# Hand-woven issue order for a linear-attention and mixture-of-experts kernel, with plainly loaded weights cast on chip

## The chip, the cores and the metric

The kernel runs on one core of one Trainium2 chip. The metric is the device time of one execution in microseconds (us). A few executions are timed for each kernel, beside executions of the kernel before on the same chip. Of each run one execution was recorded as a profile. A timed run counts as slow when it is over 1.5% above the fastest of the same kernel, and ratios use the others, the fast ones, alone. Five engines work in parallel (in the profile of the kernel before, the busy times of the first four below add up to 511.6 us in a span of 278.8): TensorE (PE; its weight loads are PEld), VectorE (DVE), ScalarE (ACT), GpSimd (POOL) and SyncE (SP, which here only issues transfers). Each has its own instruction list, and in the traces below an instruction waits behind those ahead of it in its list (in experiment 5, ScalarE's copy of kvT, whose transposes were issued at 76.9 us, stood behind casts until 83.1 us). A "session" below is one visit to one chip.

## The reference

Linear attention over 8 batches, 8 heads, 576 positions and 64 channels per head, followed by a mixture of 8 experts in which each row goes to the one expert with the largest logit. Cut to what matters:

```python
q_s = softmax(q, over channels)
k_s = softmax(k, over positions)
kv  = einsum('bhsd,bhse->bhde', k_s, v)      # 64 x 64 per head
x   = einsum('bhsd,bhde->bhse', q_s, kv)     # 4608 rows of 512
logits = x @ w_gate + modality_bias[modality_id]
e_idx  = argmax(logits)
for e in range(8):
    h = maximum(x[rows of e] @ w1[e], 0)     # 512 -> 1024
    out[rows of e] = gate * (h @ w2[e])      # 1024 -> 512
```

The modality bias decides nearly all routing, so the kernel loads only the two experts that the two biases name, and checks on chip that no row wanted another (a fallback loop handles the rest and did not run here).

## The kernel before

Each batch goes through `attend` (k, v and q are loaded in fp32, exponentiated or cast by ScalarE; 36 `kv` matmuls; the normaliser `kinv` on VectorE; transposes; gate logits; x) and `route` (ranks on VectorE). GpSimd then sends each row of x to its expert's half of a buffer `xd` in DRAM with indexed transfers, and SyncE fetches rows from it, transposed, for the FFN. An FFN "piece" is half of a y tile (4 matmuls of 512 columns) or a quarter of a 256-row first layer (8 matmuls of 256 columns). The scheduler orders every engine; the program only gives attention a higher priority.

```python
GW = 512                                     # columns of one FFN pass
GROUPS = [[0], [1], [2], [3], [4, 5], [6], [7]]

def attend(b, between=None):
    ...
    for hp in range(2):
        for j in range(NJ):                  # NJ = 9
            for hg in range(2):
                rows = slice(64 * hg, 64 * hg + 64)
                nc.tensor.matmul(out=kv[hg][:, 130 * hp : 130 * hp + 129],
                                 lhsT=ek[rows, j, ...], rhs=vb[rows, j, hp, 0:129], ...)
    kinv = small.tile([P, 2, 2], FP32, name="kinv")
    for hg in range(2):
        nc.vector.tensor_scalar_add(out=kinv[:, hg, :], in0=view(kv[hg], ...), scalar1=1e-9)
    ...                                      # kvbd = kv * kinv; transposes of q
    nc.tensor.transpose(out=kvT_ps..., in_=kvbd[:, p_, :], identity=ident)
    nc.scalar.copy(out=kvT, in_=kvT_ps...)   # ScalarE, needed by the gate matmul g
    ...

def load_weights(eid, s, wait=None):
    ld = nc.gpsimd.dma_start(out=W[...] (bf16), in_=moe_w1[...] (fp32))   # cast while loading
    ...

for ph, bs in enumerate(GROUPS):
    with tc.high_priority(offset=AHEAD):     # attention ahead of the FFN
        for b in bs:
            prep_k(b); prep_v(b, nc.scalar); prep_q(b)
            alone(attend(b))
            ...
        alone(route(ph))
        fetch(ph)
    for slot, lo, w in todo_of(ph):          # FFN passes of this phase
        ...
```

The softmax here doesn't subtract the row's maximum and nothing guards it: scores larger than these inputs give would overflow.

Of the kernel before, what the change touches and what calls it, by code (L numbers as in the profile page):

```python
# [42 lines left out]
def kernel(  # L43
# [28 lines left out]
    GW = 512  # L72
# [6 lines left out]
    GROUPS = [[0], [1], [2], [3], [4, 5], [6], [7]]  # L79
    FULL = [256, 512, 768, 1024, 1536, 1792, CAP]  # L80
# [15 lines left out]
    stage = ctx.enter_context(tc.tile_pool(name="stage", bufs=6))  # L96
    sb = ctx.enter_context(tc.tile_pool(name="sb", bufs=2))
    small = ctx.enter_context(tc.tile_pool(name="small", bufs=2))
    xpass = ctx.enter_context(tc.tile_pool(name="xpass", bufs=4))
    info = ctx.enter_context(tc.tile_pool(name="info", bufs=8))  # L100
    hbuf = ctx.enter_context(tc.tile_pool(name="hbuf", bufs=2))
# [10 lines left out]
    manual = ExitStack()  # L112

# [3 lines left out]
    def load_batch(b):  # L117
        for nm, src in (("k", k), ("v", v), ("q", q)):

            t = stage.tile([P, HG, NJ * Dh], FP32, name="st", tag="st")  # L120
            ld = nc.sync.dma_start(  # L121
                out=t,
                in_=bass.AP(
                    tensor=src.tensor,
                    offset=src.offset + b * H * S * Dh,
                    ap=[[NJ * Dh, P], [2 * S * Dh, HG], [1, NJ * Dh]],
                ),
            )
            st.setdefault(("dma", b), ld)
            st[nm, b] = t  # L130
# [7 lines left out]
    wg_sb = const.tile([P, KD, E], BF16)  # L138

    for h2 in range(2):  # L140
        for hl in range(2):
            nc.gpsimd.dma_start(
                out=wg_sb[64 * h2 : 64 * h2 + 64, 2 * hl : 2 * hl + 2, :],
                in_=bass.AP(
                    tensor=moe_w_gate.tensor,
                    offset=moe_w_gate.offset + (2 * h2 + hl) * Dh * E,
                    ap=[[E, Dh], [4 * Dh * E, 2], [1, E]],
                ),
            )
    mraw = const.tile([P, B, NJ, 2], I32)  # L150
    m32 = _dram_bitcast(moe_modality_id, I32)
    for hg in range(2):
        nc.sync.dma_start(  # L153
            out=mraw[64 * hg : 64 * hg + 64],
            in_=bass.AP(tensor=m32.tensor, offset=m32.offset, ap=[[2 * NJ, 64], [2 * S, B], [1, 2 * NJ]]),
        )
# [54 lines left out]
    xb_b = [persist.tile([P, NT2, RW], BF16, name=f"xb{i}") for i in range(2)]  # L211
    for xb in xb_b:
        nc.gpsimd.memset(xb[:, :, D + INF : RW], 0.0)
    aoff = persist.tile([P, B * NT + 1], FP32)
# [3 lines left out]

    key = const.tile([P, 2], FP32)
# [23 lines left out]
    def biases():  # L243

        modf = const.tile([P, B, NT], FP32, name="modf")
        nc.vector.memset(modf, 0.0)
        for hg in range(2):
            pr = (64 * hg, 64)
            nc.vector.tensor_copy(
                out=modf[64 * hg : 64 * hg + 64, :, 1:NT], in_=view(mraw, [[2 * NJ, B], [4, NT - 1]], 2 * hg, pr)  # L250
            )
        nc.vector.tensor_copy(out=modf[0:64, :, 0], in_=view(mraw, [[2 * NJ, B]], 2 * (NJ - 1), (0, 64)))
# [9 lines left out]
    W_dma = []  # L262

    def load_weights(eid, s, wait=None):

        for part in range(4):
            dst = W[:, s, part * 2 * F : (part + 1) * 2 * F]
            if part < 2:
                ld = nc.gpsimd.dma_start(
                    out=view(dst, [[F, 2], [1, F]]),  # L270
# [6 lines left out]
            else:  # L277
                ld = nc.gpsimd.dma_start(
                    out=view(dst, [[D, 4], [1, D]]),
# [6 lines left out]
            W_dma[:] = [ld]  # L286
            if wait is not None and part == 0:
                after(ld, [wait], "transfers in the order of need")
# [19 lines left out]
    def exp_of(b, nm, out):  # L308
        src = st.pop((nm, b))
        for g in range(2):  # L310
            nc.scalar.activation(  # L311
                out=view(out, [[Dh, 2], [HG * Dh, NJ], [1, Dh]], 2 * g * Dh),
                in_=src[:, 2 * g : 2 * g + 2, :],
                func=ACT.Exp,
            )

    def prep_k(b):
        eks[b] = sb.tile([P, NJ, HG * Dh], BF16, name="ek")
        exp_of(b, "k", eks[b])

    def prep_v(b, eng):
        vst = st.pop(("v", b))
        for hp in range(2):
            copy_on(
                eng,
                view(vb_b[b % 2], [[Dh, 2], [260, NJ], [1, Dh]], 130 * hp),
                view(vst, [[NJ * Dh, 2], [Dh, NJ], [1, Dh]], 2 * hp * NJ * Dh),
            )

    def prep_q(b):  # L330
        eqs[b] = sb.tile([P, NJ, HG * Dh], BF16, name="eq")
        exp_of(b, "q", eqs[b])

    def attend(b, between=None):
        kvbd, gx, et, vb = kvbd_b[b % 2], gx_b[b % 2], et_b[b % 2], vb_b[b % 2]
        ek, eq = eks.pop(b), eqs.pop(b)
        kv = [ka.tile([P, 512], FP32, name="kv_ps", tag="ka") for _ in range(2)]
        for hp in range(2):
            for j in range(NJ):
# [9 lines left out]
                if j == 4:  # L349
                    yield 1  # L350
            yield 1
# [7 lines left out]
        for hg in range(2):  # L359
            for h2 in range(2):  # L360
# [6 lines left out]
                )  # L367

        for c0, nj in ((0, 4), (4, 4), (8, 1)):
            tp = ka.tile([P, 1024], BF16, name="tp_ps", tag="ka")  # L370
# [12 lines left out]
            if nj > 1:  # L383
                yield 1
# [5 lines left out]
        yield 1  # L390
        if between:
            between()
# [7 lines left out]
        yield 1  # L400
# [24 lines left out]
        yield 1  # L425

        xb = xb_b[b // 2 % 2]
        o = b % 2 * NT
        nc.gpsimd.tensor_copy(out=view(xb.bitcast(I32), [[RW // 2, NT]], (o * RW + D) // 2 + 1), in_=id_i[:, b, :])
        for t in range(NT):  # L430
            T = tsz[t]
            x_ps = mm.tile([P, 512], FP32, name="x_ps", tag="mm")
            for p_ in range(NP):
                nc.tensor.matmul(  # L434
                    out=view(x_ps, [[2 * Dh, 2], [1, Dh]], (4 * (p_ % 2) + p_ // 2) * Dh, (0, T)),
                    lhsT=et[:, p_, tcol[t] : tcol[t] + T],
                    rhs=kvbd[:, p_, :],
                    start=True,
                    stop=True,
                )  # L440
            nc.vector.tensor_tensor(  # L441
                out=view(xb, [[2 * Dh, HG], [Dh, 2], [1, Dh]], (o + t) * RW, (0, T)),
                in0=view(x_ps, [[2 * Dh, HG], [Dh, 2], [1, Dh]], 0, (0, T)),
                in1=view(qi, [[1, HG], [HG, 2], [0, Dh]], t * H, (0, T)),
                op=ALU.mult,
            )
            yield t % 2

    lws, part_of = {}, {}
    ROWS = "rows of their own"  # L450

    def route(ph):
# [5 lines left out]
        xb = xb_b[b // 2 % 2]  # L458
        R2 = RW // 2
        col = (b % 2 * NT * RW + D) // 2  # L460
# [27 lines left out]
        yield 1  # L488
# [40 lines left out]
        for i in bs:  # L529
            for t in range(NT):  # L530
                c = (i - b) * NT + t
                T = tsz[t]
                w = nc.gpsimd.indirect_dma_start(  # L533
                    out=xd,
                    out_offset=bass.IndirectOffsetOnAxis(ap=place[0:T, c : c + 1], axis=0),
                    in_=xb[0:T, i % 2 * NT + t, :],
                    in_offset=None,
                    bounds_check=NSLOT - 1,
                    oob_is_err=False,
                )  # L540
                tc.declare_no_dep(w.ins, group="sent", reason=ROWS)
                tc.add_to_no_dep_group("sent", w.ins)
                part_of.setdefault(ph, []).append(w)
        yield 0
# [64 lines left out]
    def fetch(ph):  # L609
        for slot, lo, w in todo_of(ph):  # L610
# [5 lines left out]
            got["dma"] = d  # L616
# [4 lines left out]
    def ffn1(w, slot, xt, hT):  # L621

        nf = GW // w
        for f0 in range(0, KF, nf):
            h_ps = ff.tile([P, GW], FP32, name="h_ps", tag="ff")
# [51 lines left out]
    def main_pieces():  # L677

        before = None
        for ph in range(NPH):  # L680
            for slot, lo, w in todo_of(ph):
# [3 lines left out]
                if before:  # L685
                    yield from second(*before)
                before = (ph, lo, w, slot, hT, ti)
        yield from second(*before)

    main = main_pieces()  # L690

    def weave(side):
        for n in side:
            for _ in range(n):
                next(main, None)

    def alone(side):
        for _ in side:
            pass


    AHEAD = 4000
    a0 = attend(0)
    with tc.high_priority(offset=AHEAD):
        prep_k(0)
        prep_v(0, nc.scalar)
        prep_q(0)
        for _ in range(5):
            next(a0)
        gating()  # L710
    eids = nc.values_load_multi_w_load_instructions(
        eid_i[0:1, 0:2],
        engines=[ENG.Pool],
# [4 lines left out]
    load_weights(eids[0], 0)  # L718
    load_batch(2)
    after(st["dma", 2], W_dma, "transfers in the order of need")  # L720
    for ph, bs in enumerate(GROUPS):
        with tc.high_priority(offset=AHEAD):
            for b in bs:
                if b:
                    prep_k(b)
                    prep_v(b, nc.scalar)
                    prep_q(b)
                    alone(attend(b))
                else:
                    alone(a0)  # L730
                    biases()
                if ph and b + 3 < B:
                    load_batch(b + 3)
            alone(route(ph))
            if ph == 0:
                load_weights(eids[1], 1, part_of[0][-1])
            if ph == NPH - 1:
                fill_gap()
            fetch(ph)
            if ph == 0:  # L740
                load_batch(3)
                after(st["dma", 3], [got["dma"]], "transfers in the order of need")
# [89 lines left out]
```

## Time and profile before

| | before |
|---|---|
| median of the timed runs, first session | 287.61 us (286.82 to 287.75) |
| the execution that was profiled | 280.36 us, span 278.8 us |
| TensorE, VectorE, ScalarE, GpSimd busy | 194.2, 113.4, 111.3, 92.7 us |
| mean granted TensorE clock | 0.931 |

The span runs from the first instruction to the last. The profiled execution was 7 us faster than the timed ones; it is not one of them, and the record does not say in which session it was taken. The line below is from the page of the kernel before: the clock that was granted to TensorE in 40 equal slices, in tenths.

```profile
PEclk9999999999959999689979899999799999999955
```

Only a few slices fall below full speed (the clock records of this profile begin at 62.5 us; what lies before counts as full).

### The profile page before, as it was taken

What the parts mean: (1) busy time and instruction counts of PE and PEld (TensorE: products, weight loads), DVE (VectorE), ACT (ScalarE), POOL (GpSimd) and SP (SyncE); (2) the same over time, 40 slices, a digit from 0 to 9 for tenths busy, and PEclk for the clock granted to TensorE, in tenths of its full rate; (3) what the DMA queues carried; (4) which work ended last, traced back from release to release, by engine and by line L of the source; (5) the groups of instructions that cost most, each with busy time, mean ns of one, the idle gap of its engine ahead of it and who ended that gap; (6) DMA issues with size and microseconds to landing.
All of it is one profiled execution on the core that took longest, in us unless ns stands there. A gap on an engine that the chain in (4) does not pass through costs nothing.

```text
span 278.8 us, 4469 instructions
## 1 busy us (share of the span) xinstructions
PE 194.2 (70%) x1627; PEld 119.8 (43%) x1647; DVE 113.4 (41%) x415; ACT 111.3 (40%) x148; POOL 92.7 (33%) x128
## 2 busy tenths in 40 slices
PE   0242554368479899298579498994999999999400
PEld 0232333146355667167346274542446644446200
DVE  1253373525555968239728286203212221213100
ACT  1643338314378686276356122250242333331100
POOL 7610024402510171262375073273514221414200
PEclk9999999999959999689979899999799999999955
DMA  7999969796999995997994724335534220303000
GB/s 184 337 283 283 244 228 375 121 196 139 389 407 334 226 406 146 331 369 119 316 355 142 148 92 127 102 112 141 183 75 152 95 94 2 144 0 153 14 5 0
DMA packets 47580, 52.75 MB, mean 189 GB/s; under 512 B 28655, under 2 KB 30719, under 8 KB 47552
## 3 DMA queue, kind: packets, MB, share of 16 engines
q1 hardware_dynamic: 38816, 33.45, 41.0%
q0 software_dynamic: 8736, 18.95, 23.3%
q8 instruction: 15, 0.25, 0.4%
q14 instruction: 13, 0.11, 0.1%
HBM read 36.88 MB, written 15.25 MB: 187 GB/s over the span
## 4 chain that ended last, share of the span: by engine, by line
PE 37%; DMA 19%; DVE 13%; issue 13%; SPq 7%; POOL 3%; ACT 2%; POOLq 0%; DVEq 0%; ACTq 0%
PE y_ps L645 17%; PE h_ps L628 15%; DMA ti<-xd 8%; DVE xb L441 4%; DMA st<-in_v_dram 4%; SPq L572 3%; DVE y_sb L655 2%; DMA st<-in_k_dram 2%; SPq L121 2%; POOL xd L533 2%; SPq L153 2%; PE x_ps L434 2%; DMA xd<-xb,place 2%; PE tp_ps L373 1%; DVE lg L463 1%
## 5 line engine op out<-in xcount | busy, mean ns | idle before, releaser
L628 PE MATMUL h_ps<-xt,W 128*128 128x256 bf16 (+2 forms) x510 | 78.4, 305 | 9.6 <-DMA xt<-xd 7.2
L635 ACT ACTIVATE hT<-h_ps 128x512 bf16<-128x512 f32 x76 | 45.2, 596 | 90.1 <-PE h_ps L628 90.1
L645 PE MATMUL y_ps<-W,hT 128*128 128x512 bf16 x286 | 72.9, 394 | 7.7 <-DVE y_sb L655 3.6
L533 POOL DMA_INDIRECT xd<-xb,place x40 | 38.8, 970 | 86.4 <-issue 34.5
L628 PEld LDWEIGHTS <-W 128*128 128x128 bf16 x512 | 48.7, 102 | 33.5 <-issue 12.3
L658 POOL DMA_INDIRECT out_dram<-y_sb,ix x38 | 37.0, 974 | 67.2 <-DVE y_sb L655 48.0
L655 DVE TENSOR_SCALAR y_sb<-y_ps,ti 128x512 f32<-128x512 f32 x38 | 28.2, 746 | 57.2 <-PE y_ps L645 54.4
L645 PEld LDWEIGHTS <-hT 128*128 128x128 bf16 x304 | 28.7, 100 | 37.2 <-issue 6.0
L342 PE MATMUL kv_ps<-vb,ek 64*128 64x129 bf16 x288 | 16.3, 264 | 24.2 <-ACT vb L301 24.2
L441 DVE TENSOR_TENSOR xb<-x_ps,qi 128x512 bf16<-128x512 f32 (+1 forms) x40 | 25.7, 679 | 17.2 <-PE x_ps L434 17.0
L311 ACT ACTIVATE ek<-st 128x1152 bf16<-128x1152 f32 x16 | 18.1, 1159 | 18.2 <-DMA st<-in_k_dram 18.2
L311 ACT ACTIVATE eq<-st 128x1152 bf16<-128x1152 f32 x16 | 17.7, 1156 | 12.5 <-DMA st<-in_q_dram 12.5
L373 PE MATMUL tp_ps<-ident,eq 128*128 128x128 bf16 x144 | 13.8, 241 | 12.2 <-DVE kvbd L362 6.4
L301 ACT CAST vb<-st 128x1152 bf16<-128x1152 f32 x16 | 17.7, 1156 | 11.1 <-DMA st<-in_v_dram 11.1
L342 PEld LDWEIGHTS <-ek 64*128 64x128 bf16 x288 | 11.6, 115 | 23.0 <-ACT vb L301 18.9
L434 PE MATMUL x_ps<-kvbd,et 128*128 128x128 bf16 (+1 forms) x160 | 18.4, 251 | 1.1 <-DVE xb L441 0.7
L373 PEld LDWEIGHTS <-eq 128*128 128x128 bf16 x144 | 10.7, 108 | 15.9 <-issue 6.8
L434 PEld LDWEIGHTS <-et 128*128 128x128 bf16 (+1 forms) x160 | 12.0, 112 | 11.8 <-issue 9.2
L593 DVE SCALAR_TENSOR_TENSOR m<-ti,m 128x2 f32<-128x2 int32 (+2 forms) x16 | 2.4, 157 | 32.2 <-DMA ti<-xd 32.1
L301 ACT COPY et<-tp_ps 128x1024 bf16<-128x1024 bf16 x8 | 8.1, 1010 | 6.9 <-PE tp_ps L373 6.9
L362 DVE TENSOR_TENSOR kvbd<-kv_ps,kinv 64x128 bf16<-64x128 f32 x32 | 9.1, 285 | 0.6
L398 DVE CAST gx<-g_ps 64x32 bf16<-64x32 f32 x8 | 1.4, 175 | 19.3 <-PE g_ps L395 19.3
(102 smaller groups left out, 115.2 us busy)
## 6 DMA issues: line engine op xcount, KB each, us to landing
st<-in_k_dram SPq DMA_DIRECT2D x8, 1152.0 KB, 6.8
st<-in_v_dram SPq DMA_DIRECT2D x8, 1152.0 KB, 14.4
st<-in_q_dram SPq DMA_DIRECT2D x8, 1152.0 KB, 18.1
W<-in_moe_w_dram POOLq DMA_DIRECT2D x8, 512.0 KB, 12.9
xd<-xb,place POOLq DMA_INDIRECT x40, 3.5
out_dram<-y_sb,ix POOLq DMA_INDIRECT x38, 2.7
xt<-xd SPq DMA_TRANSPOSE x16, 4.8
ti<-xd SPq DMA_DIRECT2D x10, 4.0 KB, 4.1
```

What stands on the lines that cost most here:

```text
L301: nc.scalar.copy(out=out, in_=in_)
L311: nc.scalar.activation(out=view(out, [[Dh, 2], [HG * Dh, NJ], [1, Dh]], 2 * g * Dh), in_=src[:, 2 * g : 2 * g + 2, :], func=ACT.Exp,)
L342: nc.tensor.matmul(out=kv[hg][:, 130 * hp : 130 * hp + 129], lhsT=ek[rows, j, P * hp : P * hp + P], rhs=vb[rows, j, hp, 0:129], start=(j = ...
L373: nc.tensor.transpose(out=view(tp, [[2 * nj * 64, 2], [1, 64]], hp * nj * 64 + jj * 64), in_=eq[:, c0 + jj, P * hp : P * hp + P], identity ...
L434: nc.tensor.matmul(out=view(x_ps, [[2 * Dh, 2], [1, Dh]], (4 * (p_ % 2) + p_ // 2) * Dh, (0, T)), lhsT=et[:, p_, tcol[t] : tcol[t] + T], r ...
L441: nc.vector.tensor_tensor(out=view(xb, [[2 * Dh, HG], [Dh, 2], [1, Dh]], (o + t) * RW, (0, T)), in0=view(x_ps, [[2 * Dh, HG], [Dh, 2], [1, ...
L533: w = nc.gpsimd.indirect_dma_start(out=xd, out_offset=bass.IndirectOffsetOnAxis(ap=place[0:T, c : c + 1], axis=0), in_=xb[0:T, i % 2 * NT ...
L628: nc.tensor.matmul(out=h_ps[:, f * w : (f + 1) * w], lhsT=W[:, slot, kd * F + (f0 + f) * P : kd * F + (f0 + f + 1) * P], rhs=xt[:, kd, 0:w ...
L635: nc.scalar.activation(out=hT[:, f0 : f0 + nf, 0:w], in_=view(h_ps, [[w, nf], [1, w]]), func=ACT.Relu)
L645: nc.tensor.matmul(out=y_ps, lhsT=hT[:, kf, t * P : (t + 1) * P], rhs=W[:, slot, W2 + kf * D : W2 + (kf + 1) * D], start=(kf == 0), stop=( ...
L655: nc.vector.tensor_scalar(out=y_sb, in0=y_ps, scalar1=gate[:, t, 3:4], scalar2=None, op0=ALU.mult)
L658: store = nc.gpsimd.indirect_dma_start(out=out, out_offset=bass.IndirectOffsetOnAxis(ap=ix[:, t : t + 1], axis=0), in_=y_sb, in_offset=Non ...
```

## The change

The intent is to stop leaving the order to the scheduler. A `manual_schedule` region fixes every engine's list to the order in which the program emits it. `attend` and `route` yield weights (0.7, 1.5, ...) that say roughly how long the step will keep TensorE waiting. `weave` multiplies them by a rate and places an FFN piece each time a whole one is owed. Weights come as plain fp32 transfers, four on SyncE's queue and four on ScalarE's, into staging tiles, and are cast on chip. Passes are 256 wide, each batch is its own group, and more buffers are given to staging, x passes and h.

```diff
-    GW = 512
+    GW = 256
-    GROUPS = [[0], [1], [2], [3], [4, 5], [6], [7]]
+    GROUPS = [[b] for b in range(B)]
-    stage ... bufs=6     xpass ... bufs=4     hbuf ... bufs=2
+    stage ... bufs=8     xpass ... bufs=6     hbuf ... bufs=3
+    manual.enter_context(tc.manual_schedule())
...
+    def prep(b, v_eng):                     # six casts, one per step of the weave
+        for nm in "kvq":
+            for g in range(2):
+                ...
+                yield
     def attend(b):
         for hp in range(2):
             for j in range(NJ):
                 ... kv matmuls
                 if j == 4:
-                    yield 1
+                    yield 0.7
-            yield 1
+            if hp == 0:
+                yield 0.7
...
-    ld = nc.gpsimd.dma_start(out=view(dst, ...), in_=...)
+    t = stage.tile([P, HG * NJ * Dh], FP32, name="st", tag="st")
+    eng.dma_start(out=view(t, ...), in_=...)
+    def cast_weights(s, part, eng):
+        copy_on(eng, W[:, s, part * 2 * F : (part + 1) * 2 * F], wst.pop((s, part))[:, 0 : 2 * F])
...
+    def weave(side, rate, preps=()):
+        owed = 0.0
+        for x in side:
+            next(preps, None)
+            owed += x * rate
+            while owed >= 1:
+                mains(1)
+                owed -= 1
...
+    load_batch(4)
+    weave(chain(attend(2), route(2)), 0.3, prep(3, nc.scalar))
+    fetch(2)
+    load_batch(5)
+    weave(chain(attend(3), route(3)), 0.5, prep(4, nc.scalar))
+    for b in range(4, B):
+        fetch(b - 1)
+        if b + 2 < B:
+            load_batch(b + 2)
+        weave(chain(attend(b), route(b)), 0.97, prep(b + 1, nc.scalar) if b + 1 < B else ())
+    fill_gap()
+    fetch(B - 1)
+    for _ in main:
+        pass
```

## The prediction

The sum, 72 + 2 x 16 + 4 x 22.3 + 57 + 17 + 8.7, came to 275.7 (it rounded on the way).

> **What bounds the kernel now.** I read the page's strip of 40 slices first (one digit per 7 us, in tenths busy) to see whether one thing bounds the whole.
>
> ```profile
> PE   0242554368479899298579498994999999999400
> ...
> DMA  7999969796999995997994724335534220303000
> GB/s 184 337 283 283 244 228 375 121 196 139 389 407 334 226 406 146 331 369 119 316 355 142 148 92 127 102 112 141 183 75 152 95 94 2 144 0 153 14 5 0
> ```
>
> There are two regimes. For about 150 us the transfers are full and TensorE is half idle; in the last 80 us TensorE is full and the transfers are idle. Next, busy time by stretch (columns: length, then each engine's busy us and count, granted clock, DMA share, GB/s), cut where the strip changes:
>
> ```profile
> 0.00:50.00 50.00, 19.43 (x237) 14.71 (x237) 20.36 (x87) 22.55 (x23) 16.36 (x46) 1.00 0.94 270
> 50.00:100.00 50.00, 34.74 (x361) 24.61 (x363) 29.07 (x119) 24.91 (x33) 13.19 (x17) 0.93 1.02 272
> 100.00:150.00 50.00, 38.37 (x425) 25.32 (x427) 30.20 (x110) 29.86 (x37) 23.07 (x26) 0.90 0.86 273
> ...
> 195.00:262.00 67.00, 65.59 (x371) 34.34 (x376) 15.67 (x24) 21.49 (x36) 20.46 (x22) 0.97 0.28 94
> 262.00:279.00 17.00, 0.00 (x0) 0.00 (x0) 0.10 (x1) 0.00 (x0) 0.93 (x1) 0.56 0.03 8
> ```
>
> The last 17 us hold no compute: end checks and drains, which the change leaves alone. The question is how much FFN work is left when attention ends. The same view of the line that scales y tiles (38 in all) says it:
>
> ```profile
> 0.00:179.00 179.00, 11.09 (x15) 0.94 0.87 249
> 179.00:262.00 83.00, 17.07 (x23) 0.98 0.30 97
> ```
>
> 23 of 38 tiles come after 179 us. Last, the waits: who starves TensorE, and what holds the row scatters and the load queue.
>
> ```profile
> PE kv_ps L342 <- ACT vb L301: 24.2, 3, 12.4
> ...
> POOL xd L533 <- DVE et L303: 14.2, 1, 14.2
> POOL xd L533 <- DVE kvbd L362: 13.8, 1, 13.8
> ...
> SPq L572 <- DMA xd<-xb,place: 55.9, 10, 13.0
> ```
>
> The reader should see a static order that doesn't fit: TensorE stands at kv matmuls whose v has not come, while FFN pieces exist later in its program; scatters follow DVE work of another batch. From 52 us, the first FFN pass near, to 262 us TensorE is busy 173.75 of 210 us: about 36 us of idle time is what any reordering can win there.
>
> [...] while weights (GpSimd queue) and q, k, v (SP queue) ran together, the DMA share was 0.94 at 270 GB/s, no more than later. [...] The trace's 1152-element cast took 1156 ns[...].
>
> **The change part by part.**
>
> *Weights.* Before, 8 cast-loads on the GpSimd queue. Summing packet times in the trace, they used 23.9 us of all 16 engines for 8.4 MB read; q, k, v used 79.1 us for 28.3 MB, that is 2.79 us per MB. Plain weights at that rate cost 8.4 x 2.79 = 23.4 us: **no DMA time is saved**. Added are eight 2048-element casts[...]. ScalarE is 111 of 279 us busy, but they fall in the start, between 27 and 60 us, where two of them stand ahead of attention's copies. The second expert's four loads are issued by ScalarE itself; a load issue on SP took 0.37 to 4.3 us, so ScalarE is blocked for 2 to 10 us. [...]
>
> *Small loads.* The modality ids' issue took 5.17 us of SP; eight long rows replace 1024 short ones: minus 4 us early, mostly hidden behind batch 0's transfer.
>
> *Order of the start* (durations from the trace's groups). Batches 0 and 1 now load with no weights between: q1 lands near 24 us, not 35. Batch 0's scatter begins near 31 (before: 39.5). But its fetch stands in the SP queue ahead of batch 2's load, after the first weights landed near 35: the DMA idles 4 to 5 us, given back. The first FFN pieces stand after batch 1's routing: scatter and gate work end near 51, so FFN begins at about 52 to 54 (before: 58.2). Then 8 pieces (7 us), then 8 more, paired with six 1.16 us conversions and eight 0.6 us relus on ScalarE: 11.8 us. Batch 2's attention begins near 72.
>
> *Passes of 256 instead of 512.* 32 matmuls took 3.49 us at 256 columns and 6.91 at 512 in the chain's tail: the same per column. Cost zero.
>
> *The weave.* A full pass is 8 pieces, a 128-wide pass 4: 18 x 8 + 2 x 4 = 152 pieces of 8 matmuls; 3.49/4 = 0.87 us each, 132 us. One batch's yields sum to 16.4. At rates 0.3, 0.5 and 0.97 that places 4, 8 and 4 x 15 pieces beside batches 2 to 7. With the 16 before, 88 are done, and **64 are left for the tail**: 64 x 0.87 / 0.97 (clock of the tail) = 57 us. Before, 23 tiles of 4 pieces were left, 92 pieces: 80 us.
>
> *Duration of the woven stretch.* Attention's TensorE work per batch, from packed runs of the timeline: kv 1.2 to 2.1, transposes 1.3, x 1.5, logits and rest 0.8: 5.2 us. Batches 2 and 3, with 4 and 8 pieces, are bound by latency: kv, normalising 1.6, transposes and copies 4, gates 2, routing 5 on DVE, x 2: about 16 us each. Batches 4 to 7: 5.2 + 15 x 0.87 = 18.3, at a clock near 0.92 19.8, and I add 2.5 us of in-order stalls: 22.3. Other engines per batch are DVE 15, ScalarE 13.4, GpSimd 11, DMA 18: close, but under it.
>
> Sum: 72 + 2 x 16 + 4 x 22.3 = 193 for the end of attention (before: about 179 to 190), + 57 = 250, + 17 = 267. The timed median is 287.5 against a profiled span of 278.8, so I add 8.7: 275.7. My stalls are guessed on the high side where the hand-set weights look tuned (0.97, 0.3); I take 274.
>
> **The rivals.** *A: in-order stalls eat the gain.* Each engine now follows one fixed list, and a late DVE copy stops FFN pieces behind it too. For: DVE at 15 of 22 us with bursts of ten small routing instructions, three PSUM buffers. Against: the scheduler's order stalls as badly (36 us). With 6 us of stall per batch and a slower start: 288 to 295. *B: the transfers stay the bound.* If loads of a late batch still land at 146 us as before, nothing moves. Against: by my order batches 3 and 4 land near 84, batch 5 near 105, batch 6 near 118, 7 near 138, each ahead of use; the bound passes to TensorE at about 70 us. If fetches block loads longer than thought: 280 to 285. *C: the weave is near perfect.* From 52 us 163 us of TensorE work at clock 0.95 ends at 224: 241 + 8.7 = 250. It can't be reached with only 12 pieces beside batches 2 and 3.
>
> **Range and chances.** 274, with 261 to 288 for 8 in 10: the lower end takes about half of the way to rival C, the upper one rival A in its milder form. The 2% limits are 281.8 and 293.3. Faster 0.71, same 0.18, slower 0.11.
>
> **What would show it.** In the changed profile: DMA-bound strip ending near 85 to 105 us instead of 150; first FFN matmul at 50 to 55; 23 y tiles after attention become 16 (64 pieces); tail about 57 us with TensorE full; total DMA share time near 179 us as before; [...] the wait of kv for the v cast falls below 12 us. The prediction is wrong if ScalarE stands for long at its own load issues, if FFN starts after 60 us, if batches 4 to 7 take over 25 us each, or if the loads again end near 146 us.

## The result, and the profile after

In the first session the changed kernel took 303.35 us in the median of four runs (300.31 to 304.94), the kernel before 287.61. The ratio is **1.0518** (95% interval 1.0438 to 1.0597): slower. A ratio here is the mean time of one kernel's fast runs over the mean time of the other kernel's fast runs of the same rounds, so it is not quite the ratio of the medians quoted. The profile is of the run of 304.94 us, which counts as slow by a hair (1.5% above the fastest run of the four). The fast runs took 300.3 to 303.5 us, so the loss itself is not a matter of that one run.

The strips of the page of the changed kernel (40 slices of 7.6 us):

```profile
PE   0243626735826586869919967993999499999900
PEclk9999955985967579599978995998799999999975
DMA  7999689998993279269559825114312792212200
```

TensorE does not become full in the middle. Its granted clock falls again and again: between 62.5 us and the last y matmul it was at half speed for 58 us, in the kernel before for 24. The busy time by stretch, cut at the start of batch 2, of batch 4, at the end of attention and at the last y matmul (the FFN work between these two is called the tail; columns: length; busy us and count of PE, PEld, DVE, ACT, POOL; granted clock; DMA share; GB/s):

```profile
77.30:124.60 47.30, 28.31 (x275) 17.62 (x276) 23.81 (x83) 21.29 (x25) 9.96 (x12) 0.74 0.69 241
124.60:227.60 103.00, 82.04 (x785) 56.23 (x785) 53.94 (x183) 41.22 (x60) 32.85 (x39) 0.89 0.50 152
227.60:288.20 60.60, 56.27 (x404) 36.45 (x402) 18.83 (x52) 16.61 (x28) 23.04 (x24) 1.00 0.38 107
288.20:303.30 15.10, 0.16 (x1) 0.00 (x0) 2.33 (x22) 0.00 (x0) 1.15 (x2) 0.60 0.03 9
```

Attention ends at 227.6 us, not at 193. From 77.3 us that is 150.3 us for six batches, where the prediction had 121.2. The waits name something that the kernel before does not show (columns: total, times, longest):

```profile
ACT hT L641 <- remote: 25.9, 5, 7.4
DVE kinv L356 <- remote: 23.9, 5, 6.4
```

`kinv` needs nothing but TensorE's kv matmuls, yet the view of waits finds no instruction whose end explains its start and says "remote". Batch 7 shows why. First TensorE's timeline, then VectorE's (start, length, what ran, idle time before it with its releaser):

```profile
203.88 0.40 PE L342 MATMUL kv_ps<-vb,ek 64*128 64x129 bf16 x8
204.22 1.04 PE L651 MATMUL y_ps<-W,hT 128*128 128x512 bf16 x4
210.42 1.03 PE L375 MATMUL tp_ps<-ident,eq 128*128 128x128 bf16 x8 [5.17 <-DVE kvbd L363]
```
```profile
203.56 0.75 DVE L661 TENSOR_SCALAR y_sb<-y_ps,ti 128x512 f32<-128x512 f32 x1 [1.27 <-PE y_ps L651]
209.30 0.23 DVE L356 TENSOR_SCALAR kinv<-kv_ps 128x2 f32<-128x2 f32 x2 [4.99 <-remote]
```

By the records the last kv matmul of the batch ends at 204.3 us. VectorE, idle since 204.3, starts `kinv` at 209.3, TensorE stands still for 5.17 us behind it, and so does everything after it in the fixed order.

I set the trace's semaphore events against the records (a semaphore is a counter whose changes the trace lists; the events that the kv matmuls of batch 7 are paired with came at 209.3 us, where `kinv` starts). Each TensorE instruction that signals completion has a record with a modelled end and an event with the time at which the semaphore changed; the two are paired in order of time. In the profile of before, the event never came more than 0.05 us after the record's end. In the first session's profile 32 of 225 paired events came over 0.3 us late, the worst 6.47 us. All but one (0.57 us, at 166.6 us) lie in seven windows (33 to 38, 102 to 105, 128 to 131, 149 to 157, 178 to 184, 203 to 209, 232 to 241 us). The events of VectorE, ScalarE and GpSimd were on time: up to 302.9 us, behind all compute, each came within 0.04 us of the end of a record of its engine. In batch 7 the signal of the kv matmuls and that of the y matmuls issued after them both came at 209.3 us, within 0.1 us of each other, although the four y matmuls start 0.22 us apart by their records. Whatever held them back, the completions were published together. As ends are modelled, the trace cannot rule out that the last matmuls themselves ended late; that the signals came together speaks for held signals.

### The profile page after: what moved, and what is told of

Read it like the earlier page. It is cut to its first block, busy times and chain, and to the rows that moved or that the text cites. A ratio compares the mean times of both kernels' runs of the same rounds, so it can differ in the third digit from the quotient of the medians.

```text
span 303.3 us, 4861 instructions
## 1 busy us (share of the span) xinstructions
PE 202.4 (67%) x1782; PEld 137.0 (45%) x1782; DVE 129.5 (43%) x450; ACT 118.1 (39%) x153; POOL 86.9 (29%) x117
## 4 chain that ended last, share of the span: by engine, by line
PE 31%; DVE 17%; DMA 17%; issue 9%; another core or an unknown queue 9%; SPq 5%; ACT 4%; POOL 3%; POOLq 0%; ACTq 0%; DVEq 0%
PE y_ps L651 13%; PE h_ps L634 13%; DMA st<-in_k_dram 6%; DMA st<-in_q_dram 4%; DVE xb L445 4%; SPq L579 4%; DMA ti<-xd 3%; DVE y_sb L661 3%; POOL xd L539 3%; PE tp_ps L375 3%; DMA xd<-xb,place 2%; DMA out_dram<-y_sb,ix 2%; PE lg_ps L404 1%; DVE lg L466 1%
## 5 line engine op out<-in xcount | busy, mean ns | idle before, releaser
L634 PE MATMUL h_ps<-xt,W 128*128 128x256 bf16 (+1 forms) x640 | 84.5, 290 | 10.5 <-DMA xt<-xd 7.8
L634 PEld LDWEIGHTS <-W 128*128 128x128 bf16 x640 | 63.3, 106 | 25.1 <-DMA xt<-xd 8.1
L661 DVE TENSOR_SCALAR y_sb<-y_ps,ti 128x512 f32<-128x512 f32 x38 | 28.4, 749 | 60.4 <-PE y_ps L651 45.1
L375 PE MATMUL tp_ps<-ident,eq 128*128 128x128 bf16 x144 | 16.8, 287 | 22.7 <-DVE kvbd L363 21.9
L375 PEld LDWEIGHTS <-eq 128*128 128x128 bf16 x144 | 13.7, 133 | 26.2 <-DVE kvbd L363 24.2
L342 PE MATMUL kv_ps<-vb,ek 64*128 64x129 bf16 x288 | 14.4, 258 | 12.1 <-DVE vb L307 12.1
L356 DVE TENSOR_SCALAR kinv<-kv_ps 128x2 f32<-128x2 f32 x16 | 1.8, 153 | 44.6 <-remote 23.9
L305 ACT CAST vb<-st 128x1152 bf16<-128x1152 f32 x14 | 15.8, 1154 | 0.8 <-DMA st<-in_v_dram 0.8
L307 DVE COPY et<-tp_ps 128x1024 bf16<-128x1024 bf16 (+1 forms) x16 | 7.7, 489 | 16.2 <-PE tp_ps L375 14.9
L490 ACT ACTIVATE lg<-lg 128x40 f32<-128x40 f32 x8 | 1.9, 236 | 25.9 <-DVE lg L489 25.9
L305 ACT CAST W<-st 128x2048 bf16<-128x2048 f32 x6 | 11.2, 1895 | 1.5 <-DMA st<-in_moe_w_dram 1.5
```

Of the source, the lines that this page charges most:

```text
L305: nc.scalar.copy(out=out, in_=in_)
L342: nc.tensor.matmul(out=kv[hg][:, 130 * hp : 130 * hp + 129], lhsT=ek[rows, j, P * hp : P * hp + P], rhs=vb[rows, j, hp, 0:129], start=(j = ...
L375: nc.tensor.transpose(out=view(tp, [[2 * nj * 64, 2], [1, 64]], hp * nj * 64 + jj * 64), in_=eq[:, c0 + jj, P * hp : P * hp + P], identity ...
L634: nc.tensor.matmul(out=h_ps[:, f * w : (f + 1) * w], lhsT=W[:, slot, kd * F + (f0 + f) * P : kd * F + (f0 + f + 1) * P], rhs=xt[:, kd, 0:w ...
L661: nc.vector.tensor_scalar(out=y_sb, in0=y_ps, scalar1=gate[:, t, 3:4], scalar2=None, op0=ALU.mult)
```

## The experiments

Seventeen runs followed, on four chips (the record of the first session does not say which chip it had). Experiments 1 to 9 ran on one chip, 10 to 12 on a second, 13 to 15 on a third, 16 and 17 on a fourth. "Control" means the changed kernel unaltered.

### First round: what delays TensorE's completions

Two suspects stood beside the seven late windows. All of the windows lie beside a burst of indexed row sends by GpSimd. (There are eight bursts: during that of 57.6 to 65.1 us five FFN matmuls signalled on time, so a burst alone was not enough.) Six lie beside kv matmuls on 64 rows as well, five of these with FFN matmuls in between. The third suspect was the fixed order itself.

**1. The order left to the scheduler.**

```diff
-    manual.enter_context(tc.manual_schedule())
+    pass
```

> The changed kernel with its fixed order switched off, so that the scheduler orders every engine's instructions from the same program; everything else (256-wide pieces, plain weights, casts on chip) stays. Theory order (the hand order itself makes the loss: each engine waits in order behind a neighbour): the time falls back to 285-292 us, TensorE's completions come on time. Theory sends (TensorE's completion signals come 2 to 5 us late whenever GpSimd sends rows by index back to back beside the small attention matmuls): late completions appear here too wherever sends fall beside kv matmuls, and the time is open, 290-305 us. If it is over 305 us, the new parts rather than the order cost the time.

Measured: 289.91 us against 280.26 for before, ratio 1.034 (1.029 to 1.038). No completion was more than 0.05 us late.

**2. Plain sends instead of indexed ones.** Its output is wrong, which doesn't matter for the time.

```diff
-            w = nc.gpsimd.indirect_dma_start(out=xd, out_offset=IndirectOffsetOnAxis(place[...]), in_=xb[0:T, t, :], ...)
+            r0 = fixed_row(b, t)             # contiguous rows
+            w = nc.sync.dma_start(out=xd[r0 : r0 + T, :], in_=xb[0:T, t, :])
```

> Wrong result on purpose: the changed kernel with its 42 indexed row sends by GpSimd replaced by as many plain contiguous writes of the same bytes issued by SyncE, same order otherwise. Theory sends: the late completions of TensorE are gone (DVE's kinv starts within 0.5 us of the end of its kv matmuls instead of 5 to 6.5 us), woven batches shrink from 26 to about 21 us, the time to 278-285 us. Theory order or theory mixing (kv matmuls on 64 rows interleaved with FFN matmuls are what finishes late): lags and batches as before, 299-305 us.

Measured: 266.34 us, ratio 0.951 (0.947 to 0.955), no late completion.

**3. The kv matmuls in one block.**

```diff
-                if j == 4:
-                    yield 0.7
-            if hp == 0:
-                yield 0.7
...                                          # after kvbd
-        yield 1.5
+        yield 3.6
```

> The changed kernel with the 36 kv matmuls of a batch issued in one block, no FFN piece between them (the same number of pieces is placed right after the normalisation instead). Theory mixing: kinv starts within 0.5 us of the last kv matmul, batches 3 to 7 shrink by 4-5 us each, 280-288 us. Theory sends: the lag stays, because the kv block still lies beside the sends of the batch before; 297-306 us.

Measured: 257.03 us, ratio **0.916** (0.913 to 0.920), correct, no late completion.

**4. FFN pieces ahead of the attention.**

```diff
+        mains(8)                             # mains(4) ahead of batch 3
-        weave(chain(attend(b), route(b)), 0.97, ...)
+        weave(chain(attend(b), route(b)), 0.5, ...)
```

> The changed kernel with 8 FFN pieces placed ahead of each of the batches 4 to 7 (4 ahead of batch 3), while the batch before is being sent, and half the rate of pieces inside the attention. Theory sends in its narrow form (small kv matmuls beside sends): kv starts when the sends are over and shows no lag; with 7 us of FFN work in between batches stay near 22 us each, 283-292 us. In its wide form (any TensorE work beside a burst of sends is signalled late): FFN pieces show the lag instead, 295-305 us. Theory order: no gain, since kv only starts later, 300-312 us.

Measured: 297.96 us, ratio 1.064 (1.058 to 1.070), no late completion. Batches 3 to 6 took 27 to 28 us: the 8 pieces of about 0.87 us were simply added to a chain of about 20 us. Against the control (experiment 5, below) batches 3 to 5 grew by 5.8, 7.4 and 8.0 us.

This round answered less than it seemed to. Experiment 1 landed where "order" expected it. Experiments 2 and 3 came out 12 and 23 us below the lowest time that any theory had for them, which none of the theories foresaw. And experiments 1 and 4 keep both indexed sends and interleaved kv matmuls, and they had no late completion either. The lag could not belong to those suspects alone. A control was missing.

### Second round: the control

**5. The changed kernel unaltered**, and **6. FFN pieces let into kv only once**, between the two head pairs (the two `yield`s at `j == 4` removed, 2.1 in place of the 0.7 between the pairs).

> The changed kernel, unaltered, as a control beside the kernel before. The first four experiments showed no late completion of TensorE at all, although two of them keep the indexed sends and the interleaved kv matmuls. Theory kernel (the lag belongs to this exact order): 1.04 to 1.06 times the kernel before, lags of 2 to 5 us in the same six windows. Theory machine (the lag belonged to the chip or to the one execution that was profiled): no lag above 0.1 us, batches 3 to 7 of about 20 to 22 us, and 0.95 to 0.98 times the kernel before.

> The changed kernel with FFN pieces let in only once inside the kv matmuls of a batch, between the two head pairs, so no running accumulation is interrupted. Theory mixing: as fast as with the kv block whole, 0.91 to 0.93 times before. Theory sends or machine: the same as the unaltered changed kernel of this call within 1.5%.

Measured: the control took **273.29 us** (270.98 to 275.87) against 280.22 for before, ratio **0.9707** (0.9652 to 0.9763): faster. Not one completion was more than 0.05 us late: of the two expectations, that of "machine" (or of that one session) came true. Experiment 6 took 265.46 us, ratio 0.948, between its two expectations; the third round says why.

So the same program was 5% slower than before in the first session and 3% faster in this one. The same place in batch 7 of the control, TensorE and then VectorE:

```profile
184.54 0.40 PE L342 MATMUL kv_ps<-vb,ek 64*128 64x129 bf16 x8
184.88 1.04 PE L651 MATMUL y_ps<-W,hT 128*128 128x512 bf16 x4
186.10 0.62 PE L375 MATMUL tp_ps<-ident,eq 128*128 128x128 bf16 x8 [0.18 <-DVE kvbd L363]
```
```profile
184.98 0.23 DVE L356 TENSOR_SCALAR kinv<-kv_ps 128x2 f32<-128x2 f32 x2 [0.94 <-PE kv_ps L342]
```

The instructions are the same, but `kinv` starts as its kv matmuls end, and TensorE waits 0.18 us where it waited 5.17. The strips and two stretches of the control (from the start of batch 4 to the end of attention, and the tail):

```profile
PE   0243732676936678599999984999999999999700
PEclk9999965599895759689999997799999999999975
...
115.40:201.10 85.70, 78.06 (x786) 52.83 (x786) 54.09 (x183) 40.86 (x60) 33.14 (x39) 0.94 0.60 189
201.10:256.70 55.60, 55.60 (x400) 36.36 (x399) 18.51 (x51) 16.72 (x28) 22.70 (x24) 1.00 0.41 116
```

TensorE is now busy 91% of the time from batch 4 to the end of attention, and full in the tail, at a clock of 0.94 and 1.00; in the first session batches 4 to 7 had 0.89. One dip is left, at 163 to 170 us. It and the slow batches 2 and 3 are what the next round looks for.

### Third round: where the control still loses time

Why was the kv block (experiment 3) 16 us faster than the control if no completion was late in either? The waits say that the gate matmul g stood for ScalarE's copy of kvT. The wait, and ScalarE's timeline in batch 2 of the control:

```profile
PE g_ps L395 <- ACT kvT L391: 10.4, 4, 5.7
...
76.31 2.21 ACT L305 CAST vb<-st 128x1152 bf16<-128x1152 f32 x2 [0.79 <-DMA st<-in_v_dram]
80.11 1.16 ACT L325 ACTIVATE eq<-st 128x1152 bf16<-128x1152 f32 x1 [1.60 <-DMA st<-in_q_dram]
81.18 0.99 ACT L305 COPY et<-tp_ps 128x1024 bf16<-128x1024 bf16 x1
82.08 1.16 ACT L325 ACTIVATE eq<-st 128x1152 bf16<-128x1152 f32 x1
83.14 0.57 ACT L391 COPY kvT<-kvT_ps 128x512 bf16<-128x512 bf16 x1
```

The transposes that fill kvT_ps were issued at 76.9 us. The copy starts at 83.1, because in ScalarE's fixed list the six casts of the *next* batch stand ahead of it, and the cast of q waits for its transfer. The block also has three `yield`s fewer, which moved those casts three steps later. That was a second change hidden in experiment 3, and it can be made alone.

**7. Only the casts later**, kv still interleaved:

```diff
-        for x in side:
-            next(preps, None)
+        for i, x in enumerate(side):
+            if i > 2:
+                next(preps, None)
```

> The changed kernel with only this moved: the six casts of the next batch begin three steps later in the weave, so on ScalarE they no longer stand ahead of the copy of kvT; the kv matmuls stay interleaved with FFN pieces. Theory casts (the kv block helped in the third experiment because it happened to move these casts, which wait for their loads and hold back ScalarE's later copies in order): 0.915 to 0.935 times before, batch 2 about 16 us and batch 6 about 19 us instead of 21 and 26.6. Theory mixing (the interleaving itself costs): 0.96 to 0.975 times before, as the unaltered changed kernel.

**8. Only SyncE's order: loads ahead of the fetch** that waits for the sends:

```diff
-        fetch(b - 1)
         if b + 2 < B:
             load_batch(b + 2)
+        fetch(b - 1)
```
(and likewise `load_batch(5)` ahead of `fetch(2)`)

> The changed kernel with SyncE alone reordered: from batch 5 on, the loads of a batch are issued ahead of the fetch that waits for the sends, not behind it. Theory casts: ScalarE's waits for k, v and q (24 us in the control) fall under 10 us, the stalls of the kvT copy in batches 4 to 6 vanish, 0.94 to 0.96 times before; batch 2, whose casts wait for loads that this edit does not move, stays at 21 us. Theory mixing: no change, 0.965 to 0.98.

**9. The kv block and the loads first together.**

> Both edits that may help: the kv matmuls in one block and the loads ahead of the fetch. Theory casts: the block already freed ScalarE's order, so this adds at most 3 us to it: 0.905 to 0.917 times before, 254 to 257 us on a chip on which before takes 280 us. If loads behind the fetch still cost each batch 2 us, 0.88 to 0.90.

Measured, with before at 281.61 us: experiment 7 took 261.68 us, ratio 0.927 (0.913 to 0.940); experiment 8 took 268.46 us, 0.956 (0.947 to 0.965); experiment 9 took 256.28 us, 0.912 (0.904 to 0.920). ScalarE in batch 2 of experiment 7:

```profile
75.63 0.99 ACT L305 COPY et<-tp_ps 128x1024 bf16<-128x1024 bf16 x1
77.42 1.15 ACT L305 CAST vb<-st 128x1152 bf16<-128x1152 f32 x1 [0.80 <-DMA st<-in_v_dram]
78.48 0.58 ACT L391 COPY kvT<-kvT_ps 128x512 bf16<-128x512 bf16 x1
```

The copy of kvT comes at 78.5 us, ahead of the casts of q. Length of each batch, from the start of its kv matmuls to the next (us, from the start times of the records; batch 7 to its last x matmul):

```
                     b2    b3    b4    b5    b6    b7
first session       21.2  26.1  22.5  27.6  26.3  26.9
control (5)         21.2  22.4  20.4  19.2  26.6  19.5
4 FFN first         26.3  28.2  27.8  27.2  27.2  17.0
7 casts later       18.2  22.5  20.1  19.2  19.7  19.5
8 loads first       23.0  23.4  20.4  19.2  19.7  19.5
3 kv block          15.8  20.5  20.0  18.6  18.9  18.7
9 block and loads   18.0  20.2  18.7  18.6  18.9  18.7
11 fuller early     17.6  26.4  18.3  24.3  18.9  18.7
```

The 26.6 us of batch 6 has the same root, but the copy held back is ScalarE's other one, of et, the transposed q: TensorE stands 4.39 us for it, up to 167.1 us. In the control:

```profile
164.53 1.16 ACT L325 ACTIVATE eq<-st 128x1152 bf16<-128x1152 f32 x1 [1.37 <-DMA st<-in_q_dram]
...
166.08 1.00 ACT L305 COPY et<-tp_ps 128x1024 bf16<-128x1024 bf16 x1
```

Either edit removes it: the casts later, or their data earlier. Experiment 8 leaves batch 2 where it was, as expected, because its loads did not move. One of its expectations was missed: ScalarE's waits for k, v and q fell from 23.8 to 14.7 us, not below 10, since most of what is left is in the early batches. Experiment 7 missed one too: batch 2 came to 18.2 us, not about 16. Experiment 7 takes 11.6 of the 16.3 us that the block gained over the control, so the ordering of the casts is most of that gain. Interleaving inside kv costs what remains: 4.7 us by the times, about 3 by the ratios to the kernel before (0.927 against 0.916). The two were timed in different sessions, and the intervals of their ratios overlap, so this smaller part is less sure. The loads first add next to nothing to the block (257.03 and 256.28 us), as expected. Experiment 6 fits: it has two `yield`s fewer, so its casts also come later. So may experiment 2, whose batch 6 took 19.8 us: its sends of a batch were over in 3 to 4 us instead of 6 to 7, so the loads queued behind the fetch could start earlier. That reading is argued, not tested alone.

### Fourth round: other chips, and a version meant to be faster still

**10. The control again**, **11. more FFN pieces beside batches 2 and 3** (rates 0.5 and 0.75 instead of 0.3 and 0.5, on top of experiment 9), **12. the control once more**:

> The changed kernel unaltered, a third session. Nine runs on one chip showed no late completion; the first session, slower than the kernel before by 5 per cent, showed six windows of it. Theory machine: on the same chip again 0.965 to 0.98 and no lag; on another chip either state can come, and the lag windows and the slow time come together. Theory chance (any execution may fall into it): one or more of these four runs is at 295 us or more.

> A version meant to beat both kernels: kv matmuls in one block, loads ahead of the fetch, and 8 and 12 instead of 4 and 8 FFN pieces beside batches 2 and 3, where TensorE is still half idle. If those holes are free, the tail loses 8 pieces of 0.87 us and batches 2 and 3 grow by at most 3 us together: 251 to 254 us where before takes 280, ratio 0.895 to 0.905. If each piece only delays the batch that it stands in, 256 us as without it, ratio 0.91.

> The changed kernel unaltered, a fourth session, to look for the late completions of the first one again. Theory machine: most sessions show 0.965 to 0.98 and no lag, as on the two chips so far; a session with the slow state would show before near 287 us, this kernel at 300 us or more and lag windows in its profile. Theory chance: single runs at 300 us among fast ones.

Measured: the control took 273.15 us, ratio 0.972 (0.963 to 0.981), and 273.84 us (267.38 to 276.18; three of its four runs count as slow, so it has no ratio of its own). No completion was late. Experiment 11 was a miss: 265.62 us, ratio 0.946, 9 us slower than without the extra pieces. (Its profile is of a slow run of 270.30 us; the fast runs took 263.4 to 265.8, so the 9 us stand, but single lengths read from this trace are about 5 us in sum too long.) Its waits, one line:

```profile
PE h_ps L630 <- DMA xt<-xd: 21.2, 5, 6.4
```

In experiment 9 the same wait sums to 5.5 us. A piece placed early needs rows whose sends and fetch have not landed, and in a fixed list TensorE cannot step over it: batches 3 and 5 grew by 6 us each in this trace. The idle slots in the strip were not free.

### Fifth round: does the first session's state come back?

**13. The control**, **14. the kernel before unaltered**, **15. experiment 9 again**, on a third chip:

> The changed kernel unaltered, a fifth session. Theory machine: either 0.965 to 0.98 with no lag (the common state), or 1.03 to 1.06 with before near 287 us and lag windows in the trace (the first session's state).

> The kernel before, unaltered, for a trace of the same session. Ratio 0.99 to 1.01. If the session is in the first one's state, theory machine expects lag windows of over 1 us here too, since before took 287.6 us then against 280.3 us in the others; in the common state none.

> The best version so far (kv in one block, loads ahead of the fetch) in another session: 0.905 to 0.92 in the common state on any chip. In the first session's state, theory mixing expects no lag here and 0.91 to 0.93; theory sends expects lags beside the sends and 0.95 to 1.0.

Measured: 273.71 us, ratio 0.978 (0.970 to 0.986); 279.33 us, ratio 0.996; and 256.38 us, ratio **0.916** (0.910 to 0.922). No completion was late in any of the three. By the rule of 2% the control is faster in experiment 5 and unclear in 10 and 13, whose intervals reach over 0.98; all three ratios lie between 0.970 and 0.978. The state did not come back: 16 executions of the control on three chips took 267.4 to 276.2 us, against 300.3 to 304.9 in the first session. The longest lag of each profile, from the semaphore events:

```
profile                         paired  over 0.3 us  longest us
before                             200      0        0.05
changed, first session             225     32        6.47
control 5 / 10 / 12 / 13       225-229      0        0.05
before, experiment 14              198      0        0.05
all other experiments          222-230      0        0.11
```

**16 and 17. The lateness made by hand.** If late completions are the cause of the 30 us, then holding `kinv` back in a healthy session must give the first session's time. Nine VectorE operations go between kv and `kinv` in batches 3 to 7, in the control (16) and in the version of experiment 9 (17):

```diff
+        if b >= 3:
+            nc.vector.tensor_copy(out=junk[:, 0:2], in_=view(kv[1], [[130, 2]], 128))   # waits for kv
+            for _ in range(8):
+                nc.vector.tensor_tensor(out=junk, in0=junk, in1=junk, op=ALU.max)
         kinv = small.tile([P, 2, 2], FP32, name="kinv")
```

> The changed kernel with nine small VectorE operations [...] between kv and kinv in batches 3 to 7[...]: the first session's late signals made by hand. Theory path (each batch's kinv lies on the one chain that sets the length of the batch): batches 3 to 7 become 24 to 27 us as in the first session, the time 295 to 301 us, 1.05 to 1.07 times before. Theory slack (FFN work hides most of it): under 285 us, and the first session had another cause too.

> The same hand-made lateness in the version with the kv block whole and the loads first. Theory path: 256 plus 20 to 24 us, 275 to 280 us. Theory slack: here more FFN pieces stand behind the kv block, on TensorE, while VectorE is late, so less than half of it shows: 258 to 268 us.

The groups of experiment 16, then batch 7 on VectorE, then the clock strip:

```profile
L359 DVE TENSOR_TENSOR junk<-junk 128x512 f32<-128x512 f32 x40 | 27.8, 694 | 1.4
L357 DVE COPY junk<-kv_ps 128x2 f32<-128x2 f32 x5 | 0.8, 158 | 8.7 <-PE kv_ps L344 8.7
```
```profile
208.08 5.81 DVE L359 TENSOR_TENSOR junk<-junk 128x512 f32<-128x512 f32 x8
213.81 0.22 DVE L362 TENSOR_SCALAR kinv<-kv_ps 128x2 f32<-128x2 f32 x2
```
```profile
PEclk9999955989756597869996997899599999999965
```

The delay came out at (27.8 + 0.8) / 5 = 5.7 us per batch, 28.6 us in sum. Experiment 16 took **305.11 us**, ratio 1.089 (1.083 to 1.095), that is 31.8 us more than the control of experiment 5 (on another chip, with before at 279.98 and 280.22 us). Batches 3 to 7 became 28.3, 28.4, 27.3, 27.7 and 27.5 us, and the mean clock fell from 0.887 to 0.856, with the same kind of dips as in the first session. Experiment 17 took 289.07 us, ratio 1.034 (1.026 to 1.043), 32.8 us more than experiment 9. The direction of "path" holds in both, and the hope that the better version would hide half of it was wrong; but both lie above the ranges of "path" (295 to 301 and 275 to 280 us). Each microsecond of lateness made at this place cost a little over one: 31.8 / 28.6 = 1.11 in the control and 32.8 / 28.6 = 1.15 in the version of experiment 9.

The first session had less lateness at this place, 21.2 us in batches 3 to 7, and lost 21.3 us there against the control. The two agree in sum, not batch by batch: batch 6 was no longer than in the control, whose casts waited there for loads that in the first session had landed before the batch began (at 172.7 us). The rest of its 30 us lies elsewhere: in batch 1, where late signals put the gate matmul 4.2 us and the fetch of the next rows 4.7 us behind the control, and in the tail, where TensorE stood 4.1 us behind signals up to 6.45 us late. These two parts are read from the traces; no experiment made them by hand.

The clock is a likely reason for the "little over"; no run separates it. In these traces half-speed records follow long gaps of TensorE. With the 5.17 us gap that begins at 205 us of the first session, the clock records read 0.5 from 209.3 to 216.2 us. With hand-made gaps they read 0.5 from 131.2, 158.5, 185.8 and 213.1 us on, 6.8 us each, after four of the five. In the control, batch 7 has no such gap and no such record. In the 19 traces, counting gaps that began at full clock before the last y matmul, a half-speed record began within 5.3 us of the start of all 62 gaps of 2.5 us and more, and of 13 of the 18 of 2.0 to 2.4 us. So the falling clock was an effect of the stalls here, not their cause: in experiment 16 nothing but the delay was added.

## Why the prediction was right or wrong

The direction that was measured in the first session was wrong. The step of the prediction that failed is the duration of the woven stretch: "Batches 2 and 3 ... about 16 us each. Batches 4 to 7: ... and I add 2.5 us of in-order stalls: 22.3." The terms of its sum, with what each was worth in the first session and in the control of experiment 5:

| term of the sum | predicted | first session | control |
|---|---|---|---|
| batch 2's attention begins | 72 | 77.3 | 71.9 |
| batches 2 to 7 | 121.2 | 150.3 | 129.2 |
| tail | 57 | 60.5 | 55.6 |
| end checks and drains | 17 | 15.2 | 15.2 |
| time less span | 8.7 | 1.6 | 1.7 |
| sum | 275.9 | 304.9 | 273.6 |

The prediction's own sum is 275.7, as it rounded on the way.

- **The woven stretch, first session.** It was 29.1 us too long, nearly the whole error. The prediction knew late VectorE copies and late rows as causes of a stall. It did not know that TensorE's own completions could be signalled late. In batches 1 and 3 to 7 `kinv` started 1.9, 2.7, 2.0, 6.5, 5.0 and 5.0 us after its kv matmuls had ended by their records, 23.1 us in sum. Experiment 16 shows that lateness at this place costs such times. Of its own signs of being wrong, "batches 4 to 7 take over 25 us each" came true for three of the four.
- **The same stretch, healthy sessions.** There it was 8 us too long: 11.6 us too long in batches 2 and 3, and 3.5 us too short in batches 4 to 7. Part of this is rival A in a mild form, with the engine wrong: the copies that came late were ScalarE's (kvT and et behind casts that wait for loads), not VectorE's. Experiment 7 shows it, with 3 us in batch 2 and 7 us in batch 6. The rest is a mis-sized chain: batch 3, put at 16 us, took 22.4 in the control and 22.5 with the casts later, and TensorE nowhere waited over 1.4 us in it.
- **Time less span.** The 8.7 us were not an overhead. The prediction subtracted the span of a 280.36 us execution from the median of slower runs (287.5). In the profiled runs above the difference is 1.6 to 2.2 us. The error of 7 us hid the 8 us of the woven stretch, so 274 against 273.3 in the healthy sessions is partly luck. The prediction's numbers fit those sessions, not the one it was made for.
- **Weights: no DMA time saved.** Right. Their packets took 22.9 us of the 16 engines in the control (predicted 23.4, before 23.9). The casts took 1.895 us each on ScalarE and 1.222 us on VectorE.
- **Start.** Right. The first send was at 30.3 us (predicted 31), the first FFN matmul at 49.7 (52 to 54) in the control. ScalarE's four load issues took some 2.3 us in all in the first session's trace, the low end.
- **Busy time of ScalarE and VectorE.** Off the path: plus 6.6 and plus 15.9 us in the control.
- **The transfers' strip ends near 85 to 105 us.** Wrong in form. The packets of k, v and q ended at 164.1 us in the control and 172.7 in the first session, later than the 145.0 of the kernel before, because loads were queued behind fetches that wait for sends. So its sign "the loads again end near 146 us" came true. Half of rival B was in this, and what it cost came through the casts: putting the loads first (last packet at 140.4 us) was worth 5 us.
- **Tail.** Right in the control: 64 pieces, 55.6 us of full TensorE at a clock of 1.00 against the predicted 57. One reading beside it was off: 179 us is where the kernel before begins its last sends; its last x matmul ended at 165.1 us, with 27 of 38 y tiles to come, not 23. The sum does not rest on it.
- **Hand order.** Experiment 1 separates it: the new parts under the scheduler's order are 3.4% slower than before, the same parts in the hand order 2.9% faster. It is not a full test of the scheduler: the changed program no longer gives attention the high priority that the kernel before gives it, and no run put that back.

**What stays open.** Why TensorE's completions came late in the first session. All its late windows lie beside GpSimd's sends, but four controls with the same sends and the same interleaving had none, so that coincidence is not shown to be a cause. Whether the first session's chip, the hour, or something else on that machine made it cannot be told, because the state never came back. The kernel before was 2.5% slower in that session too (287.6 against 280.3 us). Whether its completions were late as well is not known, as its profile comes from a faster execution. Nor were the three other runs of the changed kernel in that session profiled; that they lost their time in the same way is inferred from their times of 300.3 to 303.5 us.

## What to carry to other kernels

In a hand-fixed order, look for the copy that the next step of the chain needs and check what stands ahead of it on its engine: moving six casts by three steps was worth 11.6 us, and keeping kv whole as well made 256 us, 8 to 9% faster than before on two chips. An idle slot on an engine is only worth filling with work whose data is surely there: experiment 11 filled such slots and took 9 us more. Before explaining a surprising time by the code, run the unchanged kernel again in another session, and check whether completion signals come when the records say the work ended.
